# Sliding-window attention block: the second of a head group's two tiles starts at token 768 instead of 1024, and its loads are merged from 24 to 12

## The chip, the cores and the metric

The kernel runs on one core of one Trainium2 chip. The metric is the device time of one execution in microseconds (us). A difference within 0.3% of it is treated as no difference.

## The reference

A transformer block over one sequence of 2048 tokens with 640 features. First comes attention with 32 heads of 20 features, in which a query sees itself and the 255 tokens before it; then a gated MLP that mixes tokens with a 2048 x 2048 matrix. The change lies in the attention part alone:

```python
H = 32; Dh = D // H; W = 256
scores = jnp.einsum("bhqd,bhkd->bhqk", q, k) * (Dh ** -0.5)
mask = (idx[:, None] - idx[None, :] >= 0) & (idx[:, None] - idx[None, :] < W)
p = _softmax(jnp.where(mask[None, None], scores, -1e9), axis=-1)
o = jnp.einsum("bhqk,bhkd->bhqd", p, v)
h = x + o.transpose(...).reshape(B, S, D) @ wo
```

The rest (layer norm, the input projection, a gelu, layer norm over half of the features, the token mixing, the gate and the output projection) comes after it.

## The kernel before

**Stages.** From the start to about 178 us of the profile the kernel normalises x, computes V, and begins the product that gives Q and K. From 178 to 241 us the rest of that product (`qk_item`, L588 to L601, called from `dense_tail`) alternates on TensorE with the first attention work. From 241 to 463 us attention runs alone. After that come the output projection and the MLP.

**How Q and K reach the attention.** Each item of `qk_item` is 128 feature rows by 512 tokens. `split_qk` (L603) cuts each value into three bf16 parts (`sg`), with work on VectorE, ScalarE and GpSimd, and one DMA (L619) stores the parts in DRAM as `qk_d`. Two bf16 make one 4-byte word there. Attention works on eight groups of four heads. A group's **stack** is a pair of SBUF tiles: tile 0 holds tokens 0 to 1023, tile 1 tokens 1024 to 2047, each for Q and K and four heads. A stack has 120 rows: six products of parts (part 0 of Q with parts 0, 1, 2 of K, part 1 with 0 and 1, part 2 with 0) times 20 features, so that one matmul over 120 rows gives a score of almost f32 accuracy. `load_stack` (L316) fills a stack with 24 DMAs of 20 rows: 2 tiles, 6 products, Q and K. The rows of product j are j, j+6, j+12 and so on. There are three stack slots, two named `slot` and one that lies in the tiles `xb`, used in turn. Three more rows (120 to 122) hold the negated maximum of each query, again in three parts, and ones on the side of K; GpSimd writes the ones once for each slot (L322), and a small DMA brings the maxima (L386).

**The attention loop** (L760 to L802) goes through 128 units u, that is 8 groups of 16 blocks of 128 tokens. Step s does

- `max_item` (L332) for unit s + 18: the scores of 128 queries with the up to 384 keys that they see. TensorE computes them in four strips of 32 queries by 288 keys, one beside the other in its columns (L359); VectorE adds the mask and takes the maximum in one pass (L369). The first 18 units are done without strips (L363), between the matmuls of `dense_tail`.
- `score_item` (L378) for unit s: transposed scores, four strips of 32 keys by 288 queries (L412), with the maxima in the extra rows; ScalarE takes the exponential (L415), GpSimd zeroes what lies outside the window (L419, L422).
- `pv_item` (L426 on) for unit s - 2: the product with V (L440). Its results leave through ScalarE or VectorE and a DMA to `o_d`.

After every eighth unit `max_rows` (L373) turns the collected maxima into rows and sends them through DRAM to the stack.

**Strips across two tiles.** `tokens` (L333) yields a range of tokens as one or two pieces, since a range may begin in tile 0 and end in tile 1. The keys of query blocks 8 and 9 do (they begin at 768 and 896), and so do the queries of key blocks 6 and 7. Because of the distance of 18 units, both fall in the same two steps of sixteen, those with s mod 16 equal to 6 and 7. There every strip is two matmuls, each with its own load of weights.

**What sets the order.** TensorE, VectorE, ScalarE and SyncE (SP) run in the order in which the code is written; GpSimd's order is set by a scheduler. All DMAs are issued by SP, in order, and a load that waits holds up what stands behind it. In the loop, `load_stack` for group g + 2 is advanced at the start of each step of group g:

```python
            for _ in range(1 + s % 2 if s >= NT else 2 * min(s, 1)):
                next(ld, None)
```

that is, 24 loads over 16 steps (L763). Stacks 0 and 1 are loaded three DMAs at a time during the projection (L719, L733, L740).

## Time and profile before

| | us |
|---|---|
| median of 3 runs | 1105.91 (1103.42 to 1106.44) |
| the profiled execution | 1106.78 |
| its span, first to last instruction | 1105.1 |
| TensorE busy | 1075.2 (97%) |
| VectorE, ScalarE, GpSimd busy | 781.0, 604.7, 314.0 |

The granted clock of TensorE is full speed in every slice. In the profile PE is TensorE's matmuls, PEld its weight loads, DVE VectorE, ACT ScalarE, POOL GpSimd, SPq SyncE's DMA queue. An idle time that is put down to "issue" is one in which the engine waited for nothing that the profile shows. A busy PE is not a PE at its peak, because matmuls are pipelined and their ends are modelled; what counts is when each step starts. A stretch of the attention loop can be cut into its steps by the start of every fourth exponential on ACT.

### The profile page before, as it was taken

Reading aid. Unit: us, or ns where it says so; the run is one execution under the profiler, and the core shown is the slowest. Engines: PE = TensorE matmul, PEld = TensorE weight load, DVE = VectorE, ACT = ScalarE, POOL = GpSimd, SP = SyncE. Lnnn points to the kernel's source line nnn. Section 1 sums busy time; section 2 is a strip of 40 time slices with the busy share of each in tenths; the row PEclk is TensorE's granted clock in tenths of the full one; section 3 lists DMA queues with packets and bytes.
Section 4 is the critical chain, followed back from the end, with each engine's and each line's share of the span. In section 5 each row is a group of like instructions: output and inputs, shape, how many; then the busy total and the mean of one; then the engine's idle time right before and its main releaser. Section 6 shows DMA issues by size and latency. Waiting matters only on the chain.

```text
span 1105.1 us, 28747 instructions
## 1 busy us (share of the span) xinstructions
PE 1075.2 (97%) x11059; PEld 968.4 (88%) x11059; DVE 781.0 (71%) x2157; ACT 604.7 (55%) x1258; POOL 314.0 (28%) x447
## 2 busy tenths in 40 slices
PE   8999999999999999999999999999999999999998
PEld 8998886658888787699999998999999899999998
DVE  6643445779999897575677668655556899987684
ACT  4443443249999899756766556443458433333331
POOL 4324446677766666721200012000001000000000
PEclk9999999999999999999999999999999999999999
DMA  7834657555565565689655342242441467684642
GB/s 252 296 115 118 175 172 262 169 181 171 190 188 189 178 192 151 183 263 296 252 184 174 131 142 77 66 133 97 127 148 51 173 223 254 229 276 137 195 141 96
DMA packets 92281, 194.73 MB, mean 176 GB/s; under 512 B 11952, under 2 KB 46272, under 8 KB 88256
## 3 DMA queue, kind: packets, MB, share of 16 engines
q1 hardware_dynamic: 92144, 192.90, 53.4%
q8 instruction: 87, 1.43, 0.6%
q14 instruction: 50, 0.41, 0.1%
HBM read 127.90 MB, written 64.95 MB: 175 GB/s over the span
## 4 chain that ended last, share of the span: by engine, by line
PE 79%; DMA 6%; ACT 4%; DVE 4%; issue 4%; POOL 2%; SPq 1%; DVEq 0%; POOLq 0%; ACTq 0%
PE g L1181 23%; PE pv L440 6%; PE bank L359 5%; PE bank L412 5%; PE zb L1066 4%; PE qk L592 4%; PE qk L594 4%; PE qk L593 4%; PE out_x L1345 3%; PE zx L1006 2%; PE out_v L1345 2%; PE zv L1006 2%; DMA h_d<-xh 1%; PE zy L1006 1%; PE zw L1006 1%
## 5 line engine op out<-in xcount | busy, mean ns | idle before, releaser
L415 ACT ACTIVATE pt<-bank 128x384 f32<-128x384 f32 (+1 forms) x452 | 180.2, 483 | 17.2 <-PE bank L412 10.8
L1181 PE MATMUL g<-zl,aw 128*128 128x432 f32 x768 | 169.1, 357 | 1.5 <-ACT zl L828 1.0
L369 DVE CUSTOM_DVE_ANT_0 junk<-bank,strip 128x288 bf16<-128x288 f32 x392 | 156.1, 452 | 12.3 <-PE bank L359 10.1
L828 ACT ACTIVATE aw<-fx 128x512 fp32r<-128x512 f32 (+2 forms) x152 | 86.2, 587 | 127.6 <-DVE fx L822 57.9
L1181 PEld LDWEIGHTS g<-zl,aw 128*128 128x128 f32 x768 | 144.0, 188 | 8.1 <-ACT zl L828 1.4
L440 PE MATMUL pv<-pt,v_sb 128*32 128x192 f32 (+3 forms) x1984 | 135.2, 322 | 4.6 <-POOL pt L419 2.4
L822 DVE TENSOR_TENSOR aw<-fx,aw 128x512 fp32r<-128x512 f32 (+2 forms) x152 | 95.8, 638 | 60.1 <-ACT aw L828 59.8
L1181 PE MATMUL g<-ze,aw 128*128 128x432 f32 x576 | 132.6, 359 | 2.3 <-DVE row L822 2.3
L1181 PEld LDWEIGHTS g<-ze,aw 128*128 128x128 f32 x576 | 107.1, 188 | 9.0 <-DVE row L822 3.7
L419 POOL TENSOR_SCALAR_AFFINE_SELECT pt<-pt 128x512 f32<-128x512 f32 x128 | 83.5, 653 | 61.2 <-ACT pt L415 59.0
L412 PE MATMUL bank<-slot 123*32 123x288 bf16 (+8 forms) x1296 | 95.7, 273 | 2.0 <-issue 1.3
L359 PE MATMUL bank<-slot 120*32 120x288 bf16 (+6 forms) x1248 | 93.5, 275 | 0.9 <-DVE mcol L369 0.8
L440 PEld LDWEIGHTS pv<-pt,v_sb 128*32 128x32 f32 x1984 | 65.5, 110 | 11.9 <-POOL pt L419 6.2
L422 POOL TENSOR_SCALAR_AFFINE_SELECT pt<-pt 128x512 f32<-128x512 f32 x112 | 71.2, 635 | 0.0
L412 PEld LDWEIGHTS <-slot 123*32 123x32 bf16 x1728 | 58.8, 96 | 13.0 <-issue 3.6
L359 PEld LDWEIGHTS <-slot 120*32 120x32 bf16 x1408 | 52.1, 95 | 15.2 <-issue 7.2
L369 DVE CUSTOM_DVE_ANT_0 junk<-bank,mask 128x384 bf16<-128x384 f32 (+2 forms) x120 | 51.2, 444 | 17.0 <-PE bank L363 15.7
L822 DVE TENSOR_TENSOR row<-g,row 128x432 f32<-128x432 f32 x80 | 48.3, 603 | 21.0 <-PE g L1181 20.6
L616 POOL TENSOR_TENSOR sg<-rest,sg 128x512 bf16<-128x512 f32 x40 | 46.7, 1167 | 56.3 <-ACT sg L615 45.6
L606 DVE TENSOR_TENSOR rest<-qk,std 128x512 f32<-128x512 f32 x40 | 27.6, 690 | 44.9 <-PE qk L594 44.9
L608 ACT ACTIVATE sg<-rest 128x512 bf16<-128x512 f32 x40 | 25.2, 631 | 54.3 <-DVE rest L606 54.3
L118 PE MATMUL wo_ps<-xb,xb 128*128 128x320 f32 x260 | 52.4, 311 | 1.5 <-DVE mvc L1460 1.5
(263 smaller groups left out, 2538.4 us busy)
## 6 DMA issues: line engine op xcount, KB each, us to landing
slot<-qk_d SPq DMA_DIRECT2D x144, 160.0 KB
fx<-wsp_in SPq DMA_DIRECT2D x32, 512.0 KB
qk_d<-sg SPq DMA_DIRECT2D x40, 384.0 KB
o_d<-ot SPq DMA_DIRECT2D x64, 128.0 KB
xb<-qk_d SPq DMA_DIRECT2D x48, 160.0 KB
fx<-hn_d SPq DMA_DIRECT2D x24, 320.0 KB
z_d<-row SPq DMA_DIRECT2D x16, 432.0 KB
g_d<-row SPq DMA_DIRECT2D x16, 432.0 KB
```

The source lines that it names most:

```text
L359: nc.tensor.matmul(ps[32 * j:32 * j + 32, o:o + w], one(st, 120, 0, hh, q0, 32), k, start=True, stop=True, tile_position=(0, 32 * j))
L369: nc.vector.tensor_tensor_reduce(out=junk[:, :n], in0=ps[:, :n], in1=keep, scale=1.0, scalar=NEG, op0=OP.add, op1=OP.max, accum_out=m_cols ...
L412: nc.tensor.matmul(ps[32 * i:32 * i + 32, b + o:b + o + w], one(st, 123, 1, hh, k0, 32), q, start=True, stop=True, tile_position=(0, 32 * i))
L415: nc.scalar.activation(pt[:, hh, :n], ps[:, :n], AF.Exp, scale=SCALE)
L419: nc.gpsimd.affine_select(out=pt[:, :, :P], in_=pt[:, :, :P], pattern=[[0, 4], [1, P]], base=0, channel_multiplier=-1, compare_op=OP.is_ge ...
L422: nc.gpsimd.affine_select(out=pt[:, :, 256:], in_=pt[:, :, 256:], pattern=[[0, 4], [-1, P]], base=-1, channel_multiplier=1, compare_op=OP. ...
L440: nc.tensor.matmul(ps[32 * hh:32 * hh + 32, a - 512 * c:b - 512 * c], v_sb[:, kb, v0:v0 + 32], pt[:, hh, a - kb * P:b - kb * P], start=fir ...
L822: (eng or nc.vector).tensor_tensor(out=out, in0=a, in1=b, op=op)
L828: nc.scalar.activation(out, a, AF.Copy)
L1006: nc.tensor.matmul(ps, a[x], b[:, y], start=start and m + x + y == 0, stop=stop and m == n - 1 and x == 1, skip_group_check=True)
L1181: nc.tensor.matmul(ps, w[m][:, x, k], zc[k][m][:, y], start=start and k + x + y == 0, stop=stop and k == 3 and x == 1, skip_group_check=True)
L1345: nc.tensor.matmul(o[b][:, :HD], l[:, x, k * P:(k + 1) * P], r[k][:, y], start=start and k + x + y == 0, stop=stop and k == 2 and x == 1, ...
```

## The change

Tile 1 of a stack now holds tokens 768 to 2047 (1280 of them), tile 0 still tokens 0 to 1023. Tokens 768 to 1023 are stored twice in DRAM and loaded twice. Query blocks from 8 on and key blocks from 6 on use tile 1, all others tile 0, so every strip is one matmul. `qk_d` becomes two DRAM tensors, and the 10 items of `split_qk` for tokens 512 to 1023 store to both (two DMAs). The maxima of tokens 768 to 1023 are sent to both tiles (one more small DMA per group). The rows of products with a common part of Q lie together, and one DMA loads 60, 40 or 20 rows: 12 DMAs per stack, of 480, 320 and 160 KB for tile 0, of 600, 400 and 200 KB for tile 1. In the loop one load is issued per step, from the first step of a group on. The loads of stack 0 come two at a time.

The diff, cut to its core (tile sizes elsewhere change with `WORDS`, in words of two bf16):

```diff
+    WORDS = (S // 4, S // 4 + P)
+    qk_d = [dram.tile([2, 3, 2 * DH, H // 2, n], F32, name=f"qk_d{b}") for b, n in enumerate(WORDS)]
...
             for b in range(2):
-                for j, parts in enumerate(((0, 0), (0, 1), (0, 2), (1, 0), (1, 1), (2, 0))):
+                row, part = (H // 2 * WORDS[b] * x for x in (1, 2 * DH))
+                for r, n, q in ((0, 3, 0), (3, 2, 1), (5, 1, 2)):
                     for a in range(2):
-                        src = qk_d[g // 4, parts[a], b, a * DH:(a + 1) * DH, g % 4 * 4:g % 4 * 4 + 4]
-                        nc.sync.dma_start(st[b][j:6 * DH:6, a], src)
+                        src = qk_d[b][g // 4, 0 if a else q, a * DH, g % 4 * 4]
+                        nc.sync.dma_start(st[b][r * DH:(r + n) * DH, a].rearrange("p h t -> p (h t)"),
+                                          bass.AP(tensor=src.tensor, offset=src.offset,
+                                                  ap=[[row, DH], [part * a, n], [1, 4 * WORDS[b]]]))
                         yield
...
-                    for o, w, k in tokens(st, 120, 1, hh, lo + skip * j, n):
-                        nc.tensor.matmul(ps[32 * j:32 * j + 32, o:o + w], one(st, 120, 0, hh, q0, 32), k,
-                                         start=True, stop=True, tile_position=(0, 32 * j))
+                    nc.tensor.matmul(ps[32 * j:32 * j + 32, :n], one(st, half_b, 120, 0, hh, q0, 32),
+                                     one(st, half_b, 120, 1, hh, lo + skip * j, n),
+                                     start=True, stop=True, tile_position=(0, 32 * j))
...
-            nc.sync.dma_start(slot_w[g % 3][b][120:123, 0], rows.rearrange("a (h r) c -> a h (r c)", h=4))
+            rows, st = rows.rearrange("a (h r) c -> a h (r c)", h=4), slot_w[g % 3]
+            if b == 0:
+                nc.sync.dma_start(st[0][120:123, 0], rows)
+                nc.sync.dma_start(st[1][120:123, 0, :, :P], rows[:, :, 6 * P // 2:])
+            else:
+                nc.sync.dma_start(st[1][120:123, 0, :, P:], rows)
...
-                for o, w, q in tokens(st, 123, 0, hh, kb * P + b, e - b):
-                    nc.tensor.matmul(ps[32 * i:32 * i + 32, b + o:b + o + w], one(st, 123, 1, hh, k0, 32), q,
-                                     start=True, stop=True, tile_position=(0, 32 * i))
+                c = int(kb > 5)
+                nc.tensor.matmul(ps[32 * i:32 * i + 32, b:e], one(st, c, 123, 1, hh, k0, 32),
+                                 one(st, c, 123, 0, hh, kb * P + b, e - b),
+                                 start=True, stop=True, tile_position=(0, 32 * i))
...
-            for _ in range(1 + s % 2 if s >= NT else 2 * min(s, 1)):
-                next(ld, None)
+            next(ld, None)
```

Three places of the built program show what moves. The first is TensorE where group 1's query block 8 and group 0's key block 6 meet (step 6). Of before (`slot_0` and `slot_1` with the numbers 1977 and 1978 are the two tiles of group 1's stack, 102 and 103 those of group 0's, `bank` is a PSUM bank):

```order
L440 MATMUL pv_1_2629<-pt_2527,v_sb 32x256 x4
L359 LDWEIGHTS slot_1_1978
L359 MATMUL bank_121<-slot_0_1977,slot_1_1978 32x256
L359 LDWEIGHTS slot_1_1978
L359 MATMUL bank_121<-slot_1_1978 32x32
...
L412 LDWEIGHTS slot_0_102
L412 MATMUL bank_123<-slot_0_102 32x256
L412 LDWEIGHTS slot_0_102
L412 MATMUL bank_123<-slot_1_103,slot_0_102 32x32
```

And now (the lines 354 and 413 are the new places of 359 and 412; the numbers of the tiles have changed by one or two):

```order
L442 MATMUL pv_1_2606<-pt_2505,v_sb 32x256 x4
L354 LDWEIGHTS slot_1_1976
L354 MATMUL bank_122<-slot_1_1976 32x288
...
L413 LDWEIGHTS slot_1_104
L413 MATMUL bank_124<-slot_1_104 32x288
```

A strip of 256 and 32 columns has become one of 288, with one weight load in place of two. Over the program that is 488 matmuls and 488 weight loads fewer.

The second place is SP in the attention loop, where group 4's stack is loaded (in before) and group 3's (now); `m_d` and its copies are the maxima, `ot` the attention output. Of before, the first part of a stack:

```order
L386 DMA slot_1_103<-m_d 3x2048
L329 DMA xb_97<-qk_d 20x2048 x3
L462 DMA o_d<-ot_3_0_5464 128x256
L329 DMA xb_97<-qk_d 20x2048
L462 DMA o_d<-ot_3_1_5548 128x256
L329 DMA xb_97<-qk_d 20x2048 x5
```

And now, from the start of a stack to the first loads of its second tile:

```order
L387 DMA xb_99<-m_d 3x4x512
L331 DMA slot_0_1975<-qk_d_64 60x1x2048 x2
L464 DMA o_d<-ot_3_0_4283 128x256
L331 DMA slot_0_1975<-qk_d_64 40x1x2048
L464 DMA o_d<-ot_3_1_4367 128x256
L331 DMA slot_0_1975<-qk_d_64 40x1x2048
L331 DMA slot_0_1975<-qk_d_64 20x2048 x2
L464 DMA o_d<-ot_0_0_4539 128x256
L331 DMA slot_1_1976<-qk_d_65 60x1x2560
```

Fewer and larger loads stand between the same stores, and the second tile's begin earlier.

The third place is GpSimd at the end of the projection, about 238 us into the profile of before: `rest` and `sg` belong to the last items of `split_qk`, `m` to the maxima of group 0, and the memset writes the ones into the second tile of the slot in `xb`. Of before:

```order
L381 CAST m_0_1_2321<-mr_1_2322 32x128
L382 TENSOR_TENSOR m_0_1_2321<-mr_1_2322,m_0_1_2321 32x128
L616 TENSOR_TENSOR sg_3_2292<-rest_3_2293,sg_3_2292 128x512
L322 MEMSET xb_98 32x2048
L610 TENSOR_TENSOR rest_3_2344<-rest_3_2344,sg_3_2343 128x512
```

And now:

```order
L377 CAST m_0_1_2301<-mr_1_2302 32x128
L323 MEMSET xb_99 32x2560
L378 TENSOR_TENSOR m_0_1_2301<-mr_1_2302,m_0_1_2301 32x128
L618 TENSOR_TENSOR sg_3_2275<-rest_3_2276,sg_3_2275 128x512
L612 TENSOR_TENSOR rest_3_2324<-rest_3_2324,sg_3_2323 128x512
```

The memset has grown by a quarter and stands two operations earlier. It may only run when TensorE has read `xb` for the last time.

## The prediction

> **What bounds the kernel now.** I read the page first, then the kernel cut into stages, then the attention loop cut into its steps, then who waits for whom there. Three stages by the view of windows (length, then busy time and instructions of PE, PEld, DVE, ACT and POOL, granted clock, DMA share, GB/s): the mixed stage, the attention loop without its last 16 units, and those.

> ```profile
> 178.00:240.90 62.90, 61.77 (x302) 38.76 (x304) 45.35 (x161) 17.88 (x29) 40.45 (x37) 1.00 0.58 194
> 240.90:440.30 199.40, 190.66 (x5747) 160.51 (x5744) 184.30 (x937) 182.37 (x475) 140.09 (x242) 1.00 0.57 178
> 440.30:463.00 22.70, 20.44 (x518) 13.26 (x511) 10.20 (x15) 22.10 (x35) 19.39 (x31) 1.00 0.68 183
> ```

> In the loop TensorE, VectorE and ScalarE are all over 91% busy: whichever is held up, the others wait. TensorE is idle for 8.7 us, VectorE for 15.1. Where that idle time lies is seen when each round of 16 steps is cut at the first exponential of a step. Steps 6 to 9 of the rounds (seven windows, their sum last):

> ```profile
> 252.17:259.71 7.54, 7.25 (x251) 6.40 (x245) 7.20 (x36) 6.95 (x18) 5.54 (x11) 1.00 0.57 180
> ...
> 364.04:374.09 10.05, 7.78 (x255) 6.75 (x250) 7.12 (x36) 7.12 (x19) 6.71 (x12) 1.00 0.52 169
> 393.96:401.32 7.36, 7.34 (x252) 6.17 (x246) 7.04 (x36) 6.89 (x18) 5.54 (x11) 1.00 0.61 196
> ...
> sum 58.71, PE 52.41 PEld 45.32 DVE 50.31 ACT 49.05 POOL 41.00; mean PE 7.49 PEld 6.47 DVE 7.19 ACT 7.01 POOL 5.86
> ```

> Two windows of steps 2 to 5, and the sum of the seven windows of steps 10 to 13:

> ```profile
> 272.80:279.69 6.89, 6.89 (x216) 5.83 (x213) 6.56 (x34) 6.81 (x19) 4.96 (x9) 1.00 0.47 137
> 300.45:307.28 6.83, 6.83 (x217) 6.00 (x214) 6.57 (x34) 6.74 (x18) 4.89 (x8) 1.00 0.47 139
> ...
> sum 47.54, PE 47.51 PEld 40.44 DVE 46.82 ACT 46.93 POOL 31.73; mean PE 6.79 PEld 5.78 DVE 6.69 ACT 6.70 POOL 4.53
> ```

> Four ordinary steps take 6.8 to 6.9 us with TensorE busy throughout. Four that hold the split strips (steps 6 and 7) take 7.36 to 10.05, on average 8.39. Who waits in the loop (total us, times, longest):

> ```profile
> ACT pt L415 <- PE bank L412: 10.5, 17, 1.4
> DVE junk L369 <- PE bank L359: 10.1, 18, 1.7
> PEld L359 <- issue: 8.3, 23, 1.4
> PEld L412 <- issue: 4.1, 8, 1.7
> PEld pv L440 <- issue: 3.2, 4, 1.5
> ```

> ScalarE and VectorE wait for TensorE some 10 us, and TensorE's weight loads wait for "issue", for nothing that the profile shows. One such place, right behind the split steps, on PE and then on ACT:

> ```profile
> 339.69 0.36 PE L359 MATMUL bank<-slot 120*32 120x288 bf16 x4
> 341.30 0.31 PE L412 MATMUL bank<-slot 123*32 123x288 bf16 x4 [1.25 <-issue]
> ...
> 341.66 2.44 ACT L415 ACTIVATE pt<-bank 128x384 f32<-128x384 f32 x6 [1.43 <-PE bank L412]
> ```

> TensorE stops between two strips of whole width for 1.25 us; no data is missing. I take it that instructions are missing. Rows for that: the DMA queues of the loop, and TensorE's instructions in steps 6 and 7 of round 5, which ran without a stop, against steps 10 and 11.

> ```profile
> DMA packets 15570, 35.55 MB, mean 178 GB/s; under 512 B 4058, under 2 KB 11517, under 8 KB 12584
> q8 instruction: 44, 0.72, 1.7%
> slot<-qk_d SPq DMA_DIRECT2D x96, 160.0 KB
> xb<-qk_d SPq DMA_DIRECT2D x48, 160.0 KB
> ...
> 393.96:397.69 3.73, 3.71 (x155) 3.39 (x150) 3.69 (x20) 3.46 (x9) 3.14 (x7) 1.00 0.64 217
> 401.32:404.68 3.36, 3.33 (x97) 2.79 (x90) 3.27 (x17) 3.27 (x9) 2.39 (x4) 1.00 0.67 200
> ```

> The loop's 44 instruction packets are 16 KB each. TensorE's 11,491 instructions make 261 per packet, so queue 8 looks like TensorE's code. Ordinary steps use (97 + 90) / 3.36 = 56 instructions per us, split steps (155 + 150) / 3.73 = 82. A packet lasts 4.7 us in ordinary steps and 3.2 in split ones. If a packet needs about 4.4 us to be replaced (3.2 and a stop of 1.25), ordinary steps just escape and split ones do not. That is my reading of the 8.39 against 6.8. [...]

> **The change part by part.**

> *Split strips.* 488 matmuls and as many weight loads go: 32 a group in `max_item`, 32 in `score_item`. As work they are worth little. Starts of whole strips of four, then of split ones:

> ```profile
> 249.97 0.31 PE L412 MATMUL bank<-slot 123*32 123x288 bf16 x4
> 250.10 0.31 PE L359 MATMUL bank<-slot 120*32 120x288 bf16 x4
> ...
> 251.50 0.27 PE L359 MATMUL bank<-slot,slot 120*32 120x256 bf16 x4
> 251.64 0.27 PE L412 MATMUL bank<-slot 123*32 123x256 bf16 x4
> ```

> 0.13 against 0.14 us: 0.01 for each of 16 sets of four in a round, 7 rounds, 1.1 us. The stops are worth more. Without them steps 6 to 9 could be as short as steps 2 to 5 (6.86). But they hold `max_rows` too: VectorE has 50.31 / 7 = 7.19 us of work there, and 6.69 in the next four steps of 6.79, so it can catch up by 0.1. I take 7.1: 58.71 - 7 x 7.1 = 9.0 us gained. The ends are 10.7 (at 6.86) and 7.2 (at 7.36, round 5's time). VectorE is what is late next.

> *The last 16 units.* They lose split strips too, but ACT is busy 22.10 of 22.70 us there: nothing.

> *The mixed stage.* Eight matmuls of `max_item` go. Starts of three, the second and third split:

> ```profile
> 205.13 0.34 PE L363 MATMUL bank<-slot 120*128 120x384 bf16 x1
> 206.02 0.28 PE L363 MATMUL bank<-slot,slot 120*128 120x256 bf16 x1
> 206.95 0.28 PE L363 MATMUL bank<-slot,slot 120*128 120x256 bf16 x1
> ```

> 0.93 against 0.89: 8 x 0.04 = 0.3 us gained.

> *The memset.* POOL's rows where the projection ends, the last read of `xb` on PE, and the wait that follows:

> ```profile
> 237.80 0.28 POOL L381 CAST m<-mr 32x128 bf16<-32x128 f32 x1 [0.30 <-DVE mr L379]
> 239.75 1.80 POOL L322 MEMSET xb<- 32x2048 f32 x1
> 244.66 0.65 POOL L419 TENSOR_SCALAR_AFFINE_SELECT pt<-pt 128x512 f32<-128x512 f32 x1
> ...
> 238.45 0.40 PE L594 MATMUL qk<-xb,wql 128*128 128x512 f32 x1
> ...
> 245.36 0.53 PE L440 MATMUL pv<-pt,v_sb 128*32 128x192 f32 x8 [0.95 <-POOL pt L419]
> ```

> The memset now stands right behind the cast, which ends at 238.08, and cannot start before 238.85: 0.77 us of waiting, and 0.45 for a quarter more. Behind it on GpSimd are the maxima, the last two items and the first mask; `pv` already waits for that mask, so 1.2 us are lost (0 if other work before it shrinks, not more than 1.2).

> *Loads, stores, SP.* 144 loads of 160 KB are 23.6 MB of the loop's 35.55; an eighth more makes 38.5 MB, 193 GB/s and a share of 0.62. No wait of the loop ends with a load, and tile 0's loads now finish earlier. SP needs 0.8 us per load and issues half as many:

> ```profile
> 160.49 2.44 SPq L329 DMA_DIRECT2D slot<-qk_d  x3
> ```

> The ten extra stores and the bunched loads of stack 1 in the mixed stage can delay an `sg` buffer. The nearest row is one wait of GpSimd there for a DMA:

> ```profile
> POOL sg L616 <- DMA slot<-qk_d: 2.3, 1, 2.3
> ```

> PE was busy 61.77 of 62.90 us in spite of it, so I take 0, at most 2.3. What larger loads do to the code packets no row shows. The longest run of loads between two stores was five (800 KB) and is now two of 480 KB, so bursts hardly grow, but tile 1's six come within six steps. I take 2 us of new stops, between 0 and 15 (rival B).

> Sum: -9.0 - 0.3 + 1.2 + 2.0 = -6.1 us. The profiled execution took 1106.78, 0.87 above the median of the runs: 1100.7 for a profiled one, 1099.8 for the median, say 1100.

> **The rivals.**

> *A: the stops stay (no difference).* They may come with the DMA traffic and not with the number of instructions. For it: one also lies in an ordinary step,

> ```profile
> 412.08 0.32 PE L440 MATMUL pv<-pt,v_sb 128*32 128x192 f32 x1 [0.33 <-issue]
> ```

> and round 5 passed its split steps without one. Against it: steps 10 to 13 have 0.03 us of idle PE in 47.54 us under the same traffic. Then only work goes: -1.1 - 0.3 + 1.2, that is 1105.7. [...] Chance with all that ends within 0.3% (3.3 us, about what a measurement of this kernel can tell): 0.20.

> *B: the merged loads starve TensorE (slower).* An ordinary packet lasts 4.7 us and its replacement takes about 4.4, so a delay of some 0.3 us is enough for a stop. A code packet that finds 480 or 600 KB queued ahead could be late by more. If two packets in each of the six rounds with loads stop TensorE for 1.25 us, that is 15 us: +15 - 9.0 - 0.3 + 1.2 = 6.9 us slower, 1112.8. It turns to slower from 8.1 us of new stops, six or seven of them. For it: the thin margin. Against it: total traffic and bursts change little, and ordinary steps ran at shares of 0.47 to 0.67 with hardly a stop. [...] Chance of slower by over 0.3%: 0.14.

> **How the numbers follow.** The forecast and its nearer ends (gain over 3.3 us) get 0.66. Low end: 10.7 + 0.3 gained and nothing lost, 1094.9, rounded to 1095. High end: past A and into the milder half of B, 2 us slower, 1108; a tenth or so stays outside above, less below.

> **What would show it.** Right: L359 and L412 without `slot,slot` rows; steps 6 to 9 at about 7.1 us in every round; "issue" waits of PEld of the loop from 15 us to under 5; about 40 packets on queue 8; VectorE's waits for L359 down; POOL's first mask about 1.2 us later after the last projection item. Wrong: steps 6 to 9 still at 8 us or more with 288-wide strips alone (A); stops that appear in steps 0 to 5, where the large loads are issued (B); a longer mixed stage.

## The result, and the profile after

The changed kernel takes 1153.1 us (median of 6 runs, 1151.6 to 1159.0), the kernel before 1104.3 beside it (6 runs, 1102.7 to 1106.4): a ratio of 1.045 [1.043, 1.047], 49 us slower. The prediction had 1100, with slower at 0.14.

The profiled execution took 1159.0 us, the slowest of the six, and spans 1157.3 against 1105.1. The three stages of the changed kernel, by the view of windows as in the prediction (the mixed stage from its first maxima on, the attention loop without its last 16 units, and those):

```profile
182.60:253.78 71.18, 64.71 (x302) 40.53 (x304) 45.67 (x164) 17.84 (x31) 39.76 (x35) 0.93 0.64 196
253.78:492.49 238.71, 203.69 (x5296) 165.73 (x5289) 187.60 (x933) 185.79 (x476) 143.18 (x244) 0.93 0.57 161
492.49:515.20 22.71, 20.68 (x486) 12.65 (x479) 9.27 (x13) 21.99 (x35) 19.25 (x31) 1.00 0.68 185
```

The loop starts 12.9 us later (253.78 for 240.90): the first maxima come 4.6 us later, and the mixed stage from there on lasts 8.3 us longer. The loop itself lasts 39.3 us longer (238.71 for 199.40). The last units are as long as before, and so is the rest. In the loop TensorE is idle for 35.0 us where it was 8.7, which is 26.3 of the 39.3. The other 13.0 are busy time: 203.69 for 190.66 us, with fewer matmuls. The granted clock goes with that; it was 1.00 and is 0.93 on average.

Cut by step, the sums of the seven windows of steps 0 to 5, of before and then of after, and two windows of steps 6 to 9 with their sum, of after:

```profile
sum 72.62, PE 70.27 PEld 57.17 DVE 68.91 ACT 70.15 POOL 48.38; mean PE 10.04 PEld 8.17 DVE 9.84 ACT 10.02 POOL 6.91
```
```profile
sum 89.54, PE 77.46 PEld 60.66 DVE 71.06 ACT 72.88 POOL 53.60; mean PE 11.07 PEld 8.67 DVE 10.15 ACT 10.41 POOL 7.66
...
299.23:306.41 7.18, 7.18 (x203) 5.97 (x202) 7.06 (x36) 6.88 (x18) 5.44 (x11) 1.00 0.70 207
...
403.42:415.46 12.04, 8.63 (x198) 7.25 (x197) 7.24 (x34) 7.33 (x17) 5.23 (x10) 0.87 0.69 204
...
sum 59.14, PE 53.55 PEld 44.79 DVE 50.09 ACT 49.11 POOL 36.62; mean PE 7.65 PEld 6.40 DVE 7.16 ACT 7.02 POOL 5.23
```

A round that isn't stopped passes steps 6 to 9 in 7.18 us: that is the 7.1 that was forecast. Another takes 12.04. And steps 0 to 5, which ran smoothly before, lose 16.9 us. The most is lost in steps 10 to 15, cut in the same way: 90.0 us where it was 68.1. So the stops are all over the round. Who waits in the loop (us in total, times, longest):

```profile
DVE junk L365 <- PE bank L354: 45.2, 36, 4.1
ACT pt L417 <- PE bank L413: 36.8, 33, 4.1
PEld L413 <- issue: 18.0, 16, 3.7
...
PE bank L413 <- DMA slot<-m_d: 10.6, 4, 3.6
...
PE bank L354 <- issue: 6.9, 3, 3.2
PE bank L413 <- issue: 6.6, 3, 3.4
```

Two kinds of stop hold TensorE up, and the other engines with it. One is old, "issue", but now up to 3.4 us long. The other is new: the scores (L413) wait for a load of the negated maxima, `slot<-m_d`. Of the 35.0 us in which TensorE is idle in the loop, eight stops called issue make 18.9, five stops for the maxima 11.4, and one stop for GpSimd's first mask 3.6. One stop of each of the two kinds on TensorE, and a window of 6.82 us that the granted clock marks, with the one behind it:

```profile
385.96 0.30 PE L354 MATMUL bank<-xb 120*32 120x288 bf16 x4
389.32 0.43 PE L413 MATMUL bank<-slot 123*32 123x288 bf16 x4 [3.06 <-DMA slot<-m_d]
...
411.54 0.30 PE L413 MATMUL bank<-slot 123*32 123x288 bf16 x2 [3.41 <-issue]
```
```profile
388.53:395.35 6.82, 6.03 (x104) 4.15 (x108) 3.92 (x17) 4.43 (x10) 1.58 (x3) 0.50 0.75 217
395.35:402.00 6.65, 6.39 (x180) 4.88 (x172) 6.29 (x32) 6.39 (x17) 4.55 (x8) 1.00 0.19 55
```

After the stop of 3.06 us TensorE runs at a clock of 0.50 for two pieces of 3.4 us, and gets 104 matmuls done where the same time holds 180. The pieces at 0.50 that begin in the loop add up to 34.1 us. So on average a stop is paid for about one and a half times: 26.3 us of it as idle time, 13.0 as slow work.

Why the maxima are late is seen on SP (SyncE). Its waits for them, in the loop of before and of after, and one instance of after:

```profile
SPq L386 <- DMA m_d<-m: 15.9, 13, 2.8
```
```profile
SPq L384 <- DMA m_d<-m: 38.8, 7, 8.2
SPq L387 <- DMA m_d<-m: 21.8, 6, 6.6
```
```profile
306.54 0.42 SPq L380 DMA_DIRECT2D m_d<-m  x1
308.14 0.35 SPq L464 DMA_DIRECT2D o_d<-ot  x1
308.54 0.79 SPq L331 DMA_DIRECT2D slot<-qk_d  x1
316.76 0.25 SPq L384 DMA_DIRECT2D xb<-m_d  x1
```

The maxima go to DRAM (L380) and come back as rows of a stack (L384, L385, L387), and the load back must wait until the store has landed. SP issues in order, so it stands still from 309.3 to 316.8, with loads of the stacks and stores of the output behind it. SP's wait for such a store was 2.8 us at most and is now up to 8.2.

The third place is the mixed stage. The longest waits there, of after:

```profile
ACT sg L610 <- DMA qk_d<-sg: 27.7, 6, 8.4
ACT sg L617 <- POOL rest L612: 27.7, 15, 5.7
POOL rest L612 <- ACT sg L610: 25.4, 6, 7.9
```

Before, ScalarE waited there for VectorE and GpSimd alone (`ACT sg L608 <- DVE rest L606` 23.6 us, 2.0 at the longest). Now it waits up to 8.4 us for an `sg` buffer whose stores haven't landed. TensorE stops for 3.4 us just ahead of that stage's first maxima and for 1.4, 3.5 and 1.5 us in it, each time waiting for VectorE, and for 3.55 us at the loop's first masks.

### The profile page after: what moved, and what is told of

It is laid out like the page before. It is cut to its first block, busy times and chain, and to the rows that moved or that the text cites. A ratio compares the mean times of both kernels' runs of the same rounds, so it can differ in the third digit from the quotient of the medians.

```text
span 1157.3 us, 27697 instructions
## 1 busy us (share of the span) xinstructions
PE 1092.2 (94%) x10571; PEld 975.7 (84%) x10571; DVE 785.4 (68%) x2157; ACT 607.6 (52%) x1258; POOL 314.1 (27%) x447
## 4 chain that ended last, share of the span: by engine, by line
PE 65%; DMA 12%; issue 8%; POOL 5%; ACT 4%; DVE 4%; SPq 1%; POOLq 0%; ACTq 0%; DVEq 0%
PE g L1187 22%; PE pv L442 5%; PE zb L1072 4%; DMA m_d<-m 4%; PE bank L413 4%; PE bank L354 3%; PE out_x L1351 3%; PE zx L1012 2%; PE qk L596 2%; PE qk L594 2%; PE qk L595 2%; PE out_v L1351 2%; PE zv L1012 2%; POOL rest L612 2%; POOL sg L618 1%
## 5 line engine op out<-in xcount | busy, mean ns | idle before, releaser
L365 DVE CUSTOM_DVE_ANT_0 junk<-bank,strip 128x288 bf16<-128x288 f32 x392 | 158.9, 453 | 42.2 <-PE bank L354 39.7
L442 PE MATMUL pv<-pt,v_sb 128*32 128x192 f32 (+3 forms) x1984 | 141.0, 336 | 10.9 <-issue 5.6
L413 PE MATMUL bank<-slot 123*32 123x288 bf16 (+6 forms) x1296 | 104.2, 301 | 17.4 <-DMA slot<-m_d 10.6
L354 PE MATMUL bank<-slot 120*32 120x288 bf16 (+2 forms) x1248 | 100.0, 300 | 8.7 <-issue 6.9
L413 PEld LDWEIGHTS <-slot 123*32 123x32 bf16 x1536 | 57.0, 102 | 33.4 <-issue 13.3
L442 PEld LDWEIGHTS pv<-pt,v_sb 128*32 128x32 f32 x1984 | 68.5, 115 | 18.7 <-POOL pt L421 9.2
L354 PEld LDWEIGHTS <-slot 120*32 120x32 bf16 x1248 | 48.9, 101 | 18.5 <-issue 9.6
L608 DVE TENSOR_TENSOR rest<-qk,std 128x512 f32<-128x512 f32 x40 | 27.5, 690 | 53.0 <-PE qk L596 40.7
```

Source lines behind the costliest of these rows:

```text
L354: nc.tensor.matmul(ps[32 * j:32 * j + 32, :n], one(st, half_b, 120, 0, hh, q0, 32), one(st, half_b, 120, 1, hh, lo + skip * j, n), start=T ...
L365: nc.vector.tensor_tensor_reduce(out=junk[:, :n], in0=ps[:, :n], in1=keep, scale=1.0, scalar=NEG, op0=OP.add, op1=OP.max, accum_out=m_cols ...
L413: nc.tensor.matmul(ps[32 * i:32 * i + 32, b:e], one(st, c, 123, 1, hh, k0, 32), one(st, c, 123, 0, hh, kb * P + b, e - b), start=True, sto ...
L442: nc.tensor.matmul(ps[32 * hh:32 * hh + 32, a - 512 * c:b - 512 * c], v_sb[:, kb, v0:v0 + 32], pt[:, hh, a - kb * P:b - kb * P], start=fir ...
```

## The experiments

**A reckoning of the code packets, for all of them.** The prediction took the stops called "issue" for missing code. The trace allows a test of that. Queue 8 (`instruction`) moves packets of 16 KB, 44 in the loop of before and 41 in that of after. I took each of them for 256 TensorE instructions, by the first finding below, to be asked for when TensorE is 321 instructions short of running dry, and to be usable 1.43 us after its transfer ends. That is my model and no view shows it; the last two numbers, and where a packet's first instruction lies, were fitted to the ten stops of the kernel before.

Two findings need no fit. They concern the stops of the matmuls that are over 0.3 us long and called issue, in the loops of before (7 of them), after (8), e2 (9) and e9 (16). In each loop these stops lie at whole multiples of 256 TensorE instructions from one another (matmuls and weight loads counted together; those of after at 408.1 and 417.9 us are 256 apart), and every one of them ends 1.3 to 1.7 us after a transfer of queue 8 has ended. The distance of 321 is less sure. It bears on the last column of the table alone, and the traces bound it on one side only: in e9 one transfer starts before TensorE is within 280 instructions of the packet's first.

With the fit, each packet's lateness follows from the trace, and can be set beside the stop that TensorE shows at just that instruction. In the loops of all the kernels below the sums agree within 1.2 us, and no single late packet is off by more than 0.4 us. In the table stand the packets that were over 0.3 us late, and how long a packet waited between being asked for and starting (median and the 90th per cent), all in us, with start and length of the loop as its first exponentials show them:

| kernel | time | start of loop | loop | late packets | lateness | stop seen there | wait to start |
|---|---|---|---|---|---|---|---|
| before | 1104.3 | 240.9 | 199.4 | 10 | 9.7 | 9.4 | 2.5, 3.7 |
| after | 1153.1 | 253.8 | 238.7 | 12 | 22.7 | 22.7 | 3.7, 7.7 |
| e1 split loads | 1135.5 | 247.5 | 220.8 | 4 | 4.4 | 4.5 | 3.1, 4.8 |
| e2 merged only | 1136.4 | 245.2 | 221.8 | 12 | 25.5 | 25.7 | 3.1, 5.6 |
| e3 split, fast | 1151.7 | 254.8 | 230.6 | 4 | 4.7 | 4.8 | 2.3, 4.8 |
| e4 merged, even | 1147.1 | 247.0 | 235.8 | 9 | 19.6 | 19.2 | 3.2, 6.5 |
| e5 late rows | 1142.6 | 255.4 | 225.6 | 7 | 16.7 | 16.6 | 3.1, 5.8 |
| e6 split, late rows | 1114.8 | 245.5 | 200.5 | 7 | 7.8 | 7.9 | 2.6, 4.5 |
| e9 merged only, even | 1123.5 | 246.1 | 224.1 | 21 | 33.1 | 32.8 | 3.2, 6.2 |
| e10 late rows, even | 1139.3 | 248.1 | 228.9 | 13 | 19.8 | 20.2 | 3.4, 6.4 |
| e12 half the strips, merged | 1198.7 | 247.6 | 284.4 | 0 | 0 | 0 | 2.1, 3.8 |
| e13 half the strips, before | 1188.2 | 241.0 | 280.1 | 0 | 0 | 0 | 1.9, 2.6 |
| e14 late rows, 40 rows | 1138.8 | 249.4 | 226.1 | 14 | 22.6 | 23.8 | 3.6, 6.5 |

Times are medians of several runs; the other columns come from one profiled execution, which can lie some us to either side (that of e9 spans 1132.8, that of e6 1108.0). The ratios below are to the kernel before, run on the same chip.

**e1_split_loads: the layout without the merging.** The new tiles, but each load of 40 or 60 rows cut into loads of 20, at the pace of before.

```
-                for r, n, q in ((0, 3, 0), (3, 2, 1), (5, 1, 2)):
-                    for a in range(2):
...
+                for r, n, q in ((0, 3, 0), (3, 2, 1), (5, 1, 2)):
+                    for j in range(n):
+                        for a in range(2):
...
+                            nc.sync.dma_start(st[b][r * DH + j:(r + n) * DH:n, a], src)
...
-            next(ld, None)
+            for _ in range(1 + s % 2 if s >= NT else 2 * min(s, 1)):
+                next(ld, None)
```

> The changed kernel's tiles, but each stack loaded by 24 DMAs of 20 rows again, at the pace of the kernel before (1.5 a step in the loop). Queue theory (a merged load puts so many bytes ahead of the small transfers that code packets, maxima and stores land late, TensorE stops for 2 to 4 us and then runs at half clock for 3.4 us): all of the loss goes and the gain of whole strips is left, 1097 us (1093 to 1103), clock 1.0. Rival layout (the larger second tile, its double stores and the maxima that go to two tiles cost the time): 1140 us or more. Rival pace: as the queue theory.

Measured 1135.5 us, 1.028 [1.022, 1.034]: a miss by 38 us. Merging isn't the whole of it; the layout costs about 32 us alone, with the gain of whole strips already in it. The late packets add up to 4.4 us only, less than before. The loss is at step 6 of the rounds instead, where tile 1 is first used, and it leads to SP again. The rows of one round on SP, then on PE, in e1 (the maxima's store is L379, the load of tile 1's row L386):

```profile
312.89 0.40 SPq L379 DMA_DIRECT2D m_d<-m  x1
313.42 0.34 SPq L463 DMA_DIRECT2D o_d<-ot  x1
314.12 1.15 SPq L332 DMA_DIRECT2D slot<-qk_d  x2
319.40 0.75 SPq L386 DMA_DIRECT2D xb<-m_d  x1
```
```profile
321.17 0.40 PE L353 MATMUL bank<-slot 120*32 120x288 bf16 x4 [1.97 <-DMA slot<-qk_d]
322.18 0.43 PE L412 MATMUL bank<-xb 123*32 123x288 bf16 x4 [0.60 <-DMA xb<-m_d]
```

The maxima were ready at 308.2, SP stored them at 312.9, waited for the store and issued the load of the row at 319.4, and TensorE needed it at 322. Before, this row was issued five to nine us ahead of its use. SP's time before, as an estimate from its rows: in a half round of 14.1 us it was issuing for 11 to 12 us (twelve loads of 0.73 us, four output stores, the maxima) and waiting up to 2.8 us for the store. It had nothing to spare. The new layout adds a load of 0.75 us a round and 25% to each row of tile 1, and SP is behind in every round from the second on.

**e2_merge_only: the merging without the layout.** Tiles, strips and maxima of before; twelve merged loads at the pace of the changed kernel.

```
-                for j, parts in enumerate(((0, 0), (0, 1), (0, 2), (1, 0), (1, 1), (2, 0))):
-                    for a in range(2):
...
+                for r, n, q in ((0, 3, 0), (3, 2, 1), (5, 1, 2)):
+                    for a in range(2):
...
+                                          bass.AP(tensor=src.tensor, offset=src.offset,
+                                                  ap=[[row, DH], [part * a, n], [1, S]]))
```

> The kernel before with its tiles of 1024 tokens and its split strips; only the loads are merged (12 a stack, 480, 320 and 160 KB) and issued at the changed kernel's pace. Queue theory: nearly all of the loss without the gain, 1150 us (1135 to 1165), TensorE at half clock again and again. Rival layout: 1104 us, as before. Rival pace: as the queue theory.

Measured 1136.4 us, 1.029 [1.024, 1.034], at the lower end of what was expected. Here SP is never late with a row, and TensorE waits for none. Its stops are nearly all called issue. In the loop of e2:

```profile
PEld L415 <- issue: 15.6, 20, 2.9
PEld L362 <- issue: 12.5, 13, 2.9
PE bank L415 <- issue: 10.7, 6, 2.7
PE bank L362 <- issue: 8.6, 4, 2.6
```

So there are two causes, and each of them alone costs some 32 us: late rows with the layout, late code packets with the merging. Together they make 49 and not 65. It may be that a TensorE that stops for one gives the other time; that isn't shown.

**e3_split_loads_fast: split loads at the changed kernel's pace.** As e1, with two loads a step (and 4 and 6 in the mixed stage, for 3).

```
-            for _ in range(1 + s % 2 if s >= NT else 2 * min(s, 1)):
+            for _ in range(2):
                 next(ld, None)
```

> The changed kernel's tiles and 24 DMAs of 20 rows, but the bytes asked for as early as in the changed kernel: two DMAs a step in the loop, four and six at a time before it. If the size of one DMA does it: within 1% of the split loads at the old pace, 1100 us. Rival pace (it is the bytes asked for in a short time, twelve steps in place of sixteen, that delay the small transfers): 1135 us or more.

Measured 1151.7 us, 1.044 [1.038, 1.049]: as slow as the changed kernel, without a merged load. Packets are late by 4.7 us only. The stops are where tile 1 is first used, as in e1, and the loop starts 7.3 us later than in e1. So bursts of short loads cost as much as merged ones in this layout, as the rival of pace had it; whether through SP's time or through the traffic isn't told apart.

**e4_merged_even_pace.** The changed kernel, with a turn without a load after each load of 60 rows.

```
                         yield
+                        if n == 3:
+                            yield
...
-            next(ld, None)
+            for _ in range(2 if s < 2 else 1):
+                next(ld, None)
```

> The changed kernel with its merged loads, each 60-row load followed by a step (or a turn) without one, so that the bytes are asked for over sixteen steps and not twelve. If the size of one DMA does it: most of the loss stays, 1130 us or more. Rival pace: the loss goes, 1105 us or less.

Measured 1147.1 us, 1.039 [1.034, 1.044]. The loop starts 6.8 us earlier than in the profile of after, and is as good as unchanged in length (235.8 for 238.7): what is gained lies in the mixed stage. It falls out as expected if the size of a load counts. But this loop has a stop of its own: at the first uses of tile 1 TensorE waits 9.5 us for loads of the stacks (`slot<-qk_d`), up to 4.8 us at a time, which it doesn't in after. So the experiment doesn't single out the size.

**e5, e6, e7: the rows' loads three steps later.** In the changed kernel, in e1 and in the kernel before, the load back of the maxima stands at step 10 and 18 in place of 7 and 15, so that SP comes to it when the store has landed.

```
-                if hh == 3 and u1 % 8 == 1 and s <= NU - LEAD + 1:
-                    next(rows)
+                if hh == 3 and u1 % 8 == 4 and s <= NU - LEAD + 4:
+                    next(rows, None)
```

> The new layout with 24 loads of 20 rows at the pace of before (as in e1_split_loads, 1135), and the rows' loads three steps later. In e1 nearly all of the loss sat at step 6 of the rounds, where TensorE waited 2 to 3 us for a row that SyncE had issued 2 to 3 us before. Theory Q: these stops go and the whole strips' gain is left, 1098 (1092 to 1108), which may be under the kernel before. Rival P, or a cost of the layout's 11% more bytes: 1130 to 1137.

e6 takes 1114.8 us, 1.010 [1.006, 1.013]. Of e1's 32 us 21 are gone, by moving one line. This is an experiment on SP's order and on nothing else: bytes, loads and layout are those of e1. Its loop, and the sum of its steps 6 to 9:

```profile
245.49:446.00 200.51, 188.68 (x5300) 155.52 (x5296) 183.89 (x937) 182.07 (x476) 140.88 (x244) 1.00 0.64 192
```
```profile
sum 50.46, PE 49.70 PEld 41.76 DVE 49.24 ACT 48.29 POOL 37.65; mean PE 7.10 PEld 5.97 DVE 7.03 ACT 6.90 POOL 5.38
```

50.46 / 7 = 7.2 us for steps 6 to 9, where the kernel before takes 8.39: the gain that was forecast is there, 8.3 us for 9.0, in the profile of the fastest of its six runs. It is given back by one row that is late (2.5 us), by packets that are late in other steps, and by 4.6 us in the mixed stage.

> The changed kernel, with one edit: the loads of the maxima rows stand three steps later in SyncE's order (step 10 and 18 of a round instead of 7 and 15), so that the store of the maxima has landed when SyncE comes to them. Theory Q (SyncE's order): the rows' loads stand behind a store that lands 6 to 8 us after its issue in this kernel, SyncE waits for it and everything behind it comes late, and TensorE stops for the rows at step 6 and 0 of a round and then runs at half clock. Then some 17 us of stops at the rows' first use and about as much at half clock go: 1120 (1108 to 1135). Rival P (code packets that land late behind large loads, no matter what SyncE waits for): the stops called issue stay and take the time, 1145 to 1153.

e5 takes 1142.6 us, 1.034 [1.030, 1.038]: 10.5 us gained for the 33 expected, nearer to the rival. SP's waits for the maxima are gone, yet rows are still late. An instance on SP and on PE in e5:

```profile
345.76 0.24 SPq L384 DMA_DIRECT2D slot<-m_d  x1
346.05 0.76 SPq L385 DMA_DIRECT2D slot<-m_d  x1
```
```profile
356.55 0.43 PE L413 MATMUL bank<-slot 123*32 123x288 bf16 x4 [2.39 <-DMA slot<-m_d]
```

Issued at 346, landed at about 356. In the trace the packets of 512 B of such a row end 8.7 us after the issue (median of the six rows with stack loads about), where in e1 and after, with SP having waited first, the medians are 1.8 and 2.1. In e6, as late but among loads of 20 rows, it is 3.4. So it is the merged loads that hold a row up, and the wait for the store had one good side: I take it that the queue of loads ran empty meanwhile.

> The kernel before with the rows' loads three steps later. Its TensorE waits at no row, so theory Q gives no change, 1104 (1100 to 1107); the 16 us that SyncE waits for stores there would be idle time without a price. If it is slower, lateness of the rows themselves costs; if faster by more than 4 us, the stops called issue hang on SyncE's bursts of loads after such a wait.

e7 takes 1103.1 us, 0.999 [0.997, 1.001]: no change, as expected. SP's waits were free as long as its rows were early.

**e8_before_row_in_4: three more issues in each half round of the kernel before.**

```
-            nc.sync.dma_start(slot_w[g % 3][b][120:123, 0], ...)
+            rows = rows.rearrange("a (h r) c -> a h (r c)", h=4)
+            for h in range(4):
+                nc.sync.dma_start(slot_w[g % 3][b][120:123, 0, h], rows[:, h])
```

> The kernel before, with each load of a maxima row cut into four loads, one for each head: the same bytes, the same layout and the same loads of the stacks, only three more issues on SyncE in each half round (0.27 us each, some 0.8 us). By the trace SyncE is busy or waiting for a store 13.9 us of each half round of 14.1, so theory Q gives late rows as in e1: 1115 to 1130. Rival P, or the layout's bytes: 1103 to 1106.

Measured 1110.1 us, 1.006 [1.004, 1.008]. The sign is the one of SP's order, the size is not: 6.4 us, where 11 to 26 were expected. SP does fall behind (it stores the maxima 4 to 7 us after they are ready, for 0 to 3 before), and TensorE stops at the first use of a tile, of tile 1 in three rounds and of tile 0 in three, but for 0.3 to 1.9 us, and the clock drops once, for 3.4 us. These delays are cheap: they are short, and nearly all are without a slow clock behind them.

**e9 and e10: merged loads spread evenly by their bytes**, e9 in the layout of before, e10 in the changed kernel with late rows.

```
-                        yield
+                        if n > 1 or a:
+                            yield
+                        if n == 3 or n == 2 and a == 0:
+                            yield
```

> As e2_merge_only (the layout of before, 12 merged loads a stack, 1136), but the loads' turns follow their bytes: 60 rows, a turn without a load, 60 rows, a turn without, 40 rows, a turn without, 40 rows, then the two of 20 rows, so that each half stack is spread over all its eight steps, as in before. Theory D (depth of the transfers' queue: loads issued faster than they land, with small transfers and code packets behind them in order): the stops go, 1106 (1100 to 1115). Rival P (a load of 480 KB holds up code packets by its mere size, at any pace): 1125 to 1137.

e9 takes 1123.5 us, 1.019 [1.013, 1.024], just under its rival's range.

> The changed kernel with both edits: rows' loads three steps later as in e5_late_rows (1143) and the loads paced by bytes as in e9. SyncE has then half the issues of before and the transfers' queue is as shallow as its bytes allow. Theory Q with D: the rows land in time and the stops called issue go; left are the later start of the maxima's stage and 11% more bytes: 1112 (1102 to 1122). Rival P: 1130 to 1143.

e10 takes 1139.3 us, 1.030 [1.027, 1.033], as its rival had it. Both are misses for the theory of depth. Pace does count for something: e9 is 13 us below e2, in their medians. But an even pace doesn't free the code packets: in e9 21 of 45 are late (its profile is of the slowest of its four runs), and the waits in its loop are these.

```profile
PEld L418 <- issue: 28.3, 20, 4.1
PE bank L418 <- issue: 21.8, 13, 3.9
```

With loads as far apart as their bytes allow, one packet in ten still waits 6.2 us or more to start. So the depth of the queue on average isn't all that counts. That a single large load in front is enough is my reading, and e9 is in line with it; no row here shows which load a packet waited behind.

**e11_late_rows_pool: the rows on GpSimd's queue.**

```
-                nc.sync.dma_start(st[0][120:123, 0], rows)
+                nc.gpsimd.dma_start(st[0][120:123, 0], rows)
```

> As e5_late_rows (1143), with the rows' loads issued by GpSimd, so on a queue of their own and not in order behind SyncE's loads of 600 KB. In e5 these small loads landed 5 to 10 us after their issue, and TensorE still waited for them at the start of a round. If the order within SyncE's queue is what delays them (theory D), they land in 2 to 3 us, the waits for rows go, and the stops called issue stay: 1130 (1122 to 1138). If the engines of the transfers are simply full, a queue of their own helps little: 1138 to 1146; GpSimd's work for the issues could cost a few us on top.

Measured 1176.7 us, 1.066 [1.062, 1.071], outside both. It answers another question than it was meant to. In GpSimd's order the load stands only one step's masks behind the maxima, not three, and GpSimd waits for the store. Its row in e11:

```profile
355.04 0.55 POOL L384 DMA_DIRECT2D slot<-m_d  x1 [7.33 <-DMA m_d<-m]
```

Four such groups of waits add up to 50 us, the masks come late, and TensorE waits for them. The rows did land sooner on this queue: the row of 6 KB 3.9 us after its issue (median of six, 1.6 to 6.9) where e5 has 8.7, though in a kernel with less traffic (151 GB/s in the loop, 171 in e5). What that is worth without GpSimd's waits stays open.

**e12 and e13: code that is needed less often**, with merged loads (e2) and with the loads of before.

```
-                for j in range(4):
-                    q0 = qb * P + 32 * j
+                for j in range(2):
+                    q0 = qb * P + 64 * j
...
-                        nc.tensor.matmul(ps[32 * j:32 * j + 32, o:o + w], one(st, 120, 0, hh, q0, 32), k,
+                        nc.tensor.matmul(ps[64 * j:64 * j + 64, o:o + w], one(st, 120, 0, hh, q0, 64), k,
```

> e2_merge_only (the layout of before, merged loads, 1136), with two strips of 64 rows and 288 columns in place of four of 32 rows for each item of the maxima in the loop: the last 32 columns of each strip are left out, so the maxima are not the reference's; VectorE's and ScalarE's work is the same. TensorE then has 16 to 20 instructions fewer in a step, about a fifth, so a code packet is needed every 5.5 us and not every 4.5 us. Theory P (the stops called issue are code packets that land late behind large loads): most of them go, 1112 (1103 to 1122). Rival (something else about large loads stops TensorE, as the data themselves): 1126 to 1137.

> The kernel before with the same strips of 64 rows, as the control of e12: the same loads as before. Theory P: the stops of steps 6 to 9 are code packets too, so they go here as well, 1096 (1091 to 1101); the gap from e13 to e12 is then well under the 33 us from before to e2. Rival: 1101 to 1106, and the gap stays near 33.

e12 takes 1198.7 us, 1.087 [1.085, 1.090], and e13 1188.2, 1.078 [1.075, 1.081]. Both times are far off, since two strips of 64 rows took TensorE longer than four of 32 (a step of the loop takes 280.13 / 112 = 2.50 us in e13, where it was 199.40 / 112 = 1.78), which I hadn't foreseen: the loop becomes TensorE's alone. But the pair answers the question better than planned. The loops of e12 and e13:

```profile
247.60:531.97 284.37, 284.30 (x4755) 133.41 (x4757) 215.21 (x933) 207.55 (x476) 142.79 (x242) 0.98 0.42 125
```
```profile
240.95:521.08 280.13, 280.08 (x4755) 132.88 (x4759) 215.36 (x937) 207.50 (x475) 140.74 (x241) 1.00 0.40 126
```

TensorE is idle for 0.1 us in either. Rounds 1 to 5 take 40.43 us each, with merged and with split loads alike; no packet is late in either. The gap that is left, 10.5 us instead of 32, is the later start (6.6) and the first round (4.3). So merged loads as such cost these rounds nothing, though code packets wait longer with them here too (3.8 us for 2.6, 90th per cent). The slower step gives slack to everything, not to the code alone; but with the lateness that the table has for e2, it fits that they cost only where TensorE uses up its code as fast as it arrives.

**e14_late_rows_max40: loads of at most 40 rows.** As e5, with 16 loads of up to 400 KB a stack, one a step.

```
-                for r, n, q in ((0, 3, 0), (3, 2, 1), (5, 1, 2)):
+                for r, n, q in ((0, 2, 0), (2, 1, 0), (3, 2, 1), (5, 1, 2)):
```

> The changed kernel with 16 loads a stack of at most 40 rows (400 KB) in place of 12 of at most 60, one a step, and the rows' loads three steps later: between e6_split_late_rows (loads of 20 rows, 1115) and e10_late_rows_even (60 rows, 1139). If the size of a load sets how late packets and rows land: 1124 (1115 to 1133). If only SyncE's time counts (16 issues instead of 24): at most 1112. If it is any merging at all: 1135 or more.

Measured 1138.8 us, 1.032 [1.029, 1.036], as e10 with 60 rows. That is the case "any merging at all" of what was expected: the cost isn't proportional to a load's size; most of it is there with 40 rows.

**e15 and e16: what the mixed stage and the rows still hold.** e15 is the changed kernel without the two loads of tile 1 that stand ahead of the projections' last stores.

```
-                if n >= 20:
+                if 20 <= n < 23:
                     for _ in range(2):
```

> The changed kernel, but behind the last of the first 24 projection items no load is issued, so that only tile 0's six loads of stack 0 stand ahead of it, as in the kernel before (half of the stack; the changed kernel has eight of twelve there). In the trace after, SyncE waits 7.0 us in one load of tile 1 for a store of the projections, with a load and stores of the projections behind it, and TensorE stops for 3.4 us at 180. If that wait delays the maxima's stage, they start 3 to 5 us earlier and the whole is 1148 (1144 to 1151). If the stores land as late whatever stands behind them: 1151 to 1155.

SP's wait for a store of the projections between 150 and 190, of after and of e15:

```profile
SPq L331 <- DMA qk_d<-sg: 7.6, 2, 7.0
```
```profile
SPq L331 <- DMA qk_d<-sg: 3.0, 1, 3.0
```

Measured 1150.6 us, 1.042 [1.038, 1.046]. The wait is shorter, the maxima start 1.0 us earlier and the loop 2.6, but the median's 2.5 us are within the intervals: inconclusive, and at most half of what was expected.

> As e6_split_late_rows (1115), with the rows' loads two steps later than in the changed kernel and not three, so 1.8 us earlier. If e6's rest comes from rows near their use (one stop of 2.5 us in its trace): 1108 to 1113. If SyncE must wait for stores again, as they land 3.9 us after their issue in the median: 1116 to 1125. If neither matters, as the rest is code packets and the later start: 1112 to 1118.

e16 (`u1 % 8 == 3` in place of 4) takes 1119.6 us, 1.011 [1.006, 1.016]: no difference from e6 that can be told. No version here beats the kernel before.

## Why the prediction was wrong

*Split strips: right.* Forecast 9.0 us gained in steps 6 to 9, with 7.1 us for the four; e6 shows 7.2 and 8.3. After has no strips across two tiles left, and its quietest rounds take 7.1 to 7.2. VectorE was named as late next; in e6 it is busy 49.24 of 50.46 us there, but TensorE 49.70, so which of them sets the 7.2 isn't shown.

*The reading of "issue" as missing code: right,* by the steps of 256 instructions and the reckoning above, and in line with e12 against e13. Rival A, that the stops belong to the traffic, falls as it was put, though the traffic bears on how late a packet is (its wait to start, 90th per cent: 2.6 us at 126 GB/s in e13, 3.7 at 178 in before, and 7.7 with the larger loads of after, at 161). By the fit, packets are late by 9.7 us in the loop of before and by 22.7 in that of after.

*Merged loads, "2 us of new stops, between 0 and 15": this step failed.* It has rival B's mechanism with the size wrong. It argued from the totals that "bursts hardly grow", and took the delay of a single packet as it was. That delay is what failed: the wait to start rises from 3.7 to 7.7 us (90th per cent), where by the fit an ordinary step leaves 5.7 us, less 2.6 for the rest of the packet's way. B priced a late packet at 1.25 us, as before; the eight long stops now cost 1.6 to 3.4, and half clock followed 64 of 67 stops over 2.6 us and 23 of 44 of 1.9 to 2.6. e2 puts this term, its quicker pace included, at 32 us: 16 times what was taken and twice its upper end. Its profile, of the fastest of four runs, has 22.4 in the loop and 4.3 ahead of it.

*"No wait of the loop ends with a load": true, and not enough.* The sum costed the bytes of stacks on the path and called them hidden. It didn't follow the small transfers that share the queue: the round trip of the maxima, SP's wait in the middle of it, and what stands behind SP. The row of that wait, 15.9 us on SP, was in the trace of before, and no part of the prediction speaks of it. SP with half the issues was booked as relief. The relief is real (7 us busy in a half round, for 11 to 12), but SP then spent it waiting for stores, up to 8.2 us at a time. e6 puts SP's order at 21 of e1's 32 us.

*The `sg` buffers, "I take 0, at most 2.3": wrong.* ScalarE waits 27.7 us for stores of `sg`, and the loop starts 12.9 us later. e1 starts its loop 6.6 us later with 0.3 us of such waits, so not all of it comes from there. Pacing the loads takes back 6.8 (e4). The memset's 1.2 us can't be told apart in that; GpSimd's first mask stops TensorE for 3.55 us in place of 0.95, and 6.8 us of half clock come with it.

*The halved clock was not in the sum.* The trace of before has none of it in the attention, where no stop of TensorE's matmuls is longer than 1.25 us, so nothing there could have priced it; any bound on a stop's cost should have been kept open above.

*What stays open.* e6 is 11 us above the kernel before; its profile shows 5.7 of them up to the loop's end, and that run is the fastest of six, 5 below the median. Why 40 rows cost as much as 60, what a queue of their own would bring the rows, and why the two causes don't add up wasn't settled.

## What to carry to other kernels

When an edit changes how loads are cut, follow the small transfers first: stores that are read back, and packets of code. Ask what is queued ahead of each, which in-order engine waits for it, and how many us lie between its landing and its first use. Waits that end just in time can mean that the queue's engine has no time to spare: SP of before issued for an estimated 11 to 12 us of each half round of 14.1 and waited up to 2.8, and three more issues of 0.27 us there cost 6.4 us in all (e8). And of these runs, merged loads cost nothing only where TensorE's steps were slower (2.50 us a step for 1.78; rounds 1 to 5 of e12, 40.43 us each as in e13); 24 short loads were the better choice here, not an oversight.
